# First transfers in written order, two squares behind their step's exponents, and own banks for the last halves of an attention and mixer kernel

## The chip, the core and the metric

The kernel runs on one core of a Trainium2 chip. The core has five engines that each take their own instructions in order: TensorE (PE, matmuls; its weight loads are listed as PEld), VectorE (DVE), ScalarE (ACT), GpSimd (POOL) and SyncE (SP, which issues DMAs).[...] The metric is the device time of one execution in microseconds (us), as the median of several executions.

## The reference

```python
# q, k, v: (8, 12, 448, 64), float32; g_q, g_k: (64,)
q_n, k_n = rmsnorm(q, g_q), rmsnorm(k, g_k)      # x / sqrt(mean(x * x) + 1e-6) * g
scores = q_n @ k_n.T / 8                         # for each batch and head
attn = softmax(scores)
x = (attn @ v), laid out as (8, 448, 768)
# w_tok1 (448, 256), w_tok2 (256, 448), w_ch1 (768, 1536), w_ch2 (1536, 768), float64
h = maximum(x.T @ w_tok1, 0) @ w_tok2
u = x + h.T
out = u + maximum(u @ w_ch1, 0) @ w_ch2          # (8, 448, 768)
```

The weights arrive as float64 and are turned into float32 by the kernel itself, from their two 32-bit words.

## The kernel before

**Units of work.** Two heads make a pair: with 64 dimensions each they fill the 128 partitions. There are 48 pairs, numbered from 0; two pairs share a "step group" `t`, so each group of four heads passes through four steps (`att_step(g)`, L650, with `t, s = divmod(g, 4)`). In a group the 448 keys are taken in seven blocks of 64. Step 0 makes the scores of block 0, steps 1 to 3 those of two blocks each (`score`, L444, matmuls at L452, exponents on ACT at L456), and from step 1 on PE also multiplies earlier blocks' exponents with the values (`values`, L525; row sums at L505). The score tiles come from a pool of four PSUM banks (`s_tile`), the other products from a pool of two (`m_tile`).

**Norms.** The norm of a pair is prepared by `square` (ACT, L1416), `reduce` (DVE, L1432), `roots` (a guess and three Newton steps, DVE or POOL) and `scale` (DVE, L1483). Then PE transposes the pair (`turn_qk`, L426), and ACT copies the result out of PSUM. In a step, the list `ahead` is issued before the step's scores and exponents, the list `behind` after them. In the first group, `turn_qk` of pairs 2 and 3 stands in step 3, between the scores and the values.

**Start.** Before the main body, the class `Start` (L1293) loads the queries and keys of pairs 0 to 3 (`load_qk`, L1377: two DMAs for the queries, two for the keys, 112 KB each) into parts of the tile `hb`. The keys of pairs 0 and 1 are issued by ACT, the rest by SP. Then it squares, reduces and scales pairs 0 and 1. Ahead of it, the kernel function loads the two gain vectors into one partition (L1516, L1517) and computes from them on DVE whether scores may grow large (L1521 to L1524). A branch on that value (`tc.If`, L1526) chooses between two bodies, `whole(tc, True, ...)` and `whole(tc, False, ...)`; with these inputs the second one runs. ACT's first activation is a one-column square (L1322), in front of which stands the load of its function table.

**Order.** PE, DVE, ACT and POOL run in written order in the whole kernel (`manual_schedule`, L1512). SP is not in that set[...].[...]

**Mixer.** Each batch's 448 by 768 result passes through the token mixing and then the channel mixing. The channel products use fewer block products than a plain multiplication: seven for the first (`ch1`, L996), fifteen forms for the second (`ch2`, L1052, matmuls at L1062). Each form `f` has two halves, `x` = 0 and 1, of 224 columns in one PSUM bank; after `x` = 1 the form's result is added to `uT` (L1077) on DVE or POOL. In the last batch the last form (f = 14) is treated apart: each half is added directly to the left half of one row block of `uT`, block 1 or block 4 (L1081). While a batch is mixed, the attention of the following batch is interleaved with it.

**End.** In the last batch, four of the six row blocks of `uT` are turned on DVE (L1090) and stored (L773). The last two, 1 and 4, go through `turn_last` (L1092): PE transposes (L1099) the right half (`lo` = 2), an engine copies it out of the bank (L1102, L1104), a DMA stores it (L1105), and then the same for the left half (`lo` = 0), in the same bank.

Of the kernel before, what the change touches and what calls it, by code (L numbers as in the profile page):

```python
# [8 lines left out]
F32 = mybir.dt.float32  # L9
# [14 lines left out]
NF9 = 15  # L24
# [59 lines left out]
def whole(ctx, tc, shifted, pre, q, k, v, g_q, g_k, moe_w_tok1, moe_w_tok2, moe_w_ch1, moe_w_ch2, out):  # L84


    nc = tc.nc
    B, H, S, D = q.shape
    C = H * D
    DT = moe_w_tok1.shape[1]  # L90
# [559 lines left out]
    def att_step(g):  # L650
# [54 lines left out]
        ahead, sooner, behind, turns = [], [], [], []  # L705
        f = lambda fn, *pairs: [lambda i=i: fn(i, st) for i in pairs]
        scales = lambda n: [lambda i=i: scale(i) for i in (n, n + 1)]
        if g in (1, 5):
            ahead, behind = f(pre.square, g // 4 * 2 + 4), f(pre.reduce, g // 4 * 2 + 4)
        elif g in (2, 6):  # L710
            ahead, behind = f(pre.square, g // 4 * 2 + 5), f(pre.reduce, g // 4 * 2 + 5)
        elif g in (3, 7):
            behind = pre.roots(g // 4 * 2 + 4, st)
        elif g in (4, 8):
            behind = scales(g // 4 * 2 + 2)
# [336 lines left out]
    def ch2(b, f, x):  # L1052

        put_off_done()
        if x == 0:
            st["m"] = m_tile()
        ps = st["m"]
        for i in range(4):
# [30 lines left out]
        t = st["y", cc] = turn_pool.tile([P, S], F32, name="turned")  # L1089
        nc.vector.transpose(out=t[:], in_=st["uT", b][:, cc, :])  # L1090

    def turn_last(b, cc, eng):  # L1092

        ps = s_tile("t_ps")
        t = cv_sb[:, cc // KC].rearrange("r (c n) -> r c n", c=NS)
        dst = out[b][:, cc * P:(cc + 1) * P].rearrange("(c r) n -> r c n", r=R)
        for lo in (HN, 0):
            for c in range(lo, lo + HN):
                nc.tensor.transpose(ps[0:R, c * P:(c + 1) * P], st["uT", b][:, cc, c * R:(c + 1) * R], ident[:])  # L1099
            part = ps[0:R, lo * P:(lo + HN) * P].rearrange("r (c n) -> r c n", c=HN)  # L1100
            if lo and cc == 1:
                nc.scalar.copy(out=t[0:R, lo:lo + HN], in_=part)  # L1102
            else:
                nc.vector.tensor_copy(out=t[0:R, lo:lo + HN], in_=part)  # L1104
            eng.dma_start(out=dst[:, lo:lo + HN], in_=t[0:R, lo:lo + HN])  # L1105

    def turns(b, cs, send=True):

# [65 lines left out]
    def last_items(b, items):  # L1174

        if ending(b):
            l = [(0.3, lambda cc=cc: (trans_y(b, cc), send_y(b, cc, st.pop(("y", cc))))) for cc in y_order(b)[:4]]
            last = [(0.1, lambda: turn_last(b, 1, nc.sync)), (0.1, lambda: turn_last(b, 1 + KC, nc.scalar))]
            return (items[:4] + l[0:1] + items[4:6] + l[1:2] + items[6:11] + l[2:3] + items[11:12] + l[3:4]
                    + items[12:] + last)  # L1180
        l = turns(b, y_order(b)[:4], not in_next(b))
        if b == 1:
            return merge(items, l)
        return items[:2] + [l[0]] + items[2:5] + [l[1]] + items[5:8] + [l[2]] + items[8:10] + [l[3], items[10]]
# [108 lines left out]
class Start:  # L1293


    def __init__(self, ctx, tc, q, k, g_q, g_k, w2):
        self.nc = nc = tc.nc
        self.q, self.k = q, k
        B, H, S, D = q.shape
# [19 lines left out]

        warm = const.tile([P, 1], F32, name="warm")  # L1320
        nc.vector.memset(warm[:], 1.0)
        nc.scalar.activation(out=warm[:], in_=warm[:], func=AF.Square)  # L1322
        self.load_qk(0, self.st, other=nc.scalar)
        self.load_qk(1, self.st, other=nc.scalar)
        self.g_t = const.tile([P, 2], F32, name="g_t")
        for i, g in enumerate((g_q, g_k)):
            for a in range(2):
# [164 lines left out]
@with_exitstack  # L1492
def kernel(
    ctx: ExitStack,
    tc: tile.TileContext,
    q: bass.AP,
    k: bass.AP,
    v: bass.AP,
    g_q: bass.AP,
    g_k: bass.AP,  # L1500
    moe_w_tok1: bass.AP,
    moe_w_tok2: bass.AP,
    moe_w_ch1: bass.AP,
    moe_w_ch2: bass.AP,
    out: bass.AP,
):


    nc = tc.nc
    D = q.shape[-1]  # L1510
    args = (q, k, v, g_q, g_k, moe_w_tok1, moe_w_tok2, moe_w_ch1, moe_w_ch2, out)
    ctx.enter_context(tc.manual_schedule(engines={  # L1512
        e.engine for e in (nc.tensor, nc.vector, nc.scalar, nc.gpsimd)}))
    gate = ctx.enter_context(tc.tile_pool(name="gate", bufs=1))
    g2 = gate.tile([1, 2, D], F32, name="g2")
    nc.sync.dma_start(out=g2[:, 0, :], in_=g_q.rearrange("(o d) -> o d", o=1))  # L1516
    nc.scalar.dma_start(out=g2[:, 1, :], in_=g_k.rearrange("(o d) -> o d", o=1))  # L1517
    gg = gate.tile([1, D], F32, name="gg")
    most = gate.tile([1, 1], F32, name="most")
    large = gate.tile([1, 1], I32, name="large")  # L1520
    nc.vector.tensor_tensor(out=gg[:], in0=g2[:, 0, :], in1=g2[:, 1, :], op=ALU.mult)  # L1521
    nc.vector.tensor_tensor(out=gg[:], in0=gg[:], in1=gg[:], op=ALU.mult)
    nc.vector.tensor_reduce(out=most[:], in_=gg[:], axis=AX_X, op=ALU.max)
    nc.vector.tensor_scalar(large[:], most[:], SCORE_BOUND**2 / D, None, ALU.is_gt)  # L1524
    pre = Start(ctx, tc, q, k, g_q, g_k, moe_w_ch2)
    with tc.If(nc.values_load(large[0:1, 0:1], min_val=0, max_val=1,  # L1526
                              skip_runtime_bounds_check_because="a comparison's result") > 0) as arm:
        whole(tc, True, pre, *args)
    with arm.Else():
        whole(tc, False, pre, *args)  # L1530
# [30 lines left out]
```

## Time and profile before

| | |
|---|---|
| Median of three runs | 1285.62 us (1283.6 to 1289.3) |
| Profiled execution, own time | 1289.21 us |
| Its span, first to last instruction | 1287.4 us |
| PE busy | 1253.8 us (97%) |
| DVE busy | 798.1 us (62%) |
| ACT busy | 392.7 us (31%) |
| POOL busy | 386.8 us (30%) |
| DMA | 228.37 MB, mean 177 GB/s |
| Chain that ended last | PE 86%, DVE 4%, DMA 4%, SP's queue 2%, ACT 1% |
| Mean granted PE clock | 0.995 |

All of it comes from one profiled execution. The span counts from the first to the last instruction; the execution's own time has some 1.8 us around it. "Busy" leaves out what an engine's queue does alone: waiting, branching and issuing DMAs. A line number names the line of the kernel before. A row of a view in order of time gives start, duration, engine, line, operation, what it writes and reads, its shape, a count, and in brackets how long the engine stood idle before it and what released it. A wait for several semaphores is put down to the one that came last, which can be a wait of another instruction just before.

### The profile page before, as it was taken

What the parts mean: (1) busy time and instruction counts of PE and PEld (TensorE: products, weight loads), DVE (VectorE), ACT (ScalarE), POOL (GpSimd) and SP (SyncE); (2) the same over time, 40 slices, a digit from 0 to 9 for tenths busy, and PEclk for the clock granted to TensorE, in tenths of its full rate; (3) what the DMA queues carried; (4) which work ended last, traced back from release to release, by engine and by line L of the source; (5) the groups of instructions that cost most, each with busy time, mean ns of one, the idle gap of its engine ahead of it and who ended that gap; (6) DMA issues with size and microseconds to landing.
All of it is one profiled execution on the core that took longest, in us unless ns stands there. A gap on an engine that the chain in (4) does not pass through costs nothing.

```text
span 1287.4 us, 20019 instructions
## 1 busy us (share of the span) xinstructions
PE 1253.8 (97%) x7236; PEld 889.2 (69%) x7236; DVE 798.1 (62%) x1243; ACT 392.7 (31%) x783; POOL 386.8 (30%) x629
## 2 busy tenths in 40 slices
PE   4999999999999999999999999999999999999997
PEld 2444444447744477796788768885887867797997
DVE  6889878846774255864668356765558456554233
ACT  3664333223331044302443034311343024300210
POOL 1112443024896612331133122241122322131222
PEclk9999999999999899999999999999999999999999
DMA  8676595999799867595657867595866864386554
GB/s 160 178 197 176 142 248 141 213 243 243 222 264 231 190 160 170 143 247 118 160 162 158 208 142 185 133 216 126 189 156 150 228 137 137 118 209 153 178 172 92
DMA packets 490112, 228.37 MB, mean 177 GB/s; under 512 B 371860, under 2 KB 450580, under 8 KB 490004
## 3 DMA queue, kind: packets, MB, share of 16 engines
q1 hardware_dynamic: 483154, 214.13, 67.4%
q0 software_dynamic: 3584, 12.06, 3.0%
q10 hardware_dynamic: 3266, 0.80, 0.3%
q8 instruction: 59, 0.97, 0.3%
q14 instruction: 49, 0.40, 0.1%
HBM read 184.26 MB, written 42.66 MB: 176 GB/s over the span
## 4 chain that ended last, share of the span: by engine, by line
PE 86%; DVE 4%; DMA 4%; SPq 2%; ACT 1%; issue 1%; DVEq 0%; ACTq 0%
PE m_ps L996 25%; PE m_ps L1062 21%; PE s_ps L452 9%; PE o_ps L525 9%; PE m_ps L876 5%; PE m_ps L966 5%; PE m_ps L1045 4%; PE m_ps L834 2%; PE t_ps L834 2%; PE d_ps L505 1%; DMA raw<-wp 1%; PE m_ps L505 1%; DVE raw L345 1%; DVE raw L343 1%; DMA x<-xs 1%
## 5 line engine op out<-in xcount | busy, mean ns | idle before, releaser
L1062 PE MATMUL m_ps<-hb,unit 128*128 128x224 f32 x1440 | 277.5, 354 | 1.2 <-DVE uT L1081 1.2
L1062 PEld LDWEIGHTS m_ps<-hb,unit 128*128 128x128 f32 x1440 | 270.9, 190 | 10.4 <-issue 7.5
L996 PE MATMUL m_ps<-tu,unit 128*128 128x224 f32 x1008 | 201.6, 355 | 1.3 <-ACT r L1006 1.3
L996 PEld LDWEIGHTS m_ps<-tu,unit 128*128 128x128 f32 x1008 | 189.1, 190 | 15.0 <-issue 9.2
L456 ACT ACTIVATE e<-s_ps 128x448 f32<-128x448 f32 x294 | 138.5, 553 | 178.4 <-PE s_ps L452 170.1
L996 PE MATMUL m_ps<-uT,unit 128*128 128x224 f32 x756 | 151.2, 354 | 0.1
L996 PEld LDWEIGHTS m_ps<-uT,unit 128*128 128x128 f32 x756 | 142.2, 190 | 7.2 <-issue 3.9
L452 PE MATMUL s_ps<-qkT 64*64 64x448 f32 x1260 | 143.8, 545 | 0.8 <-ACT x L816 0.8
L525 PE MATMUL o_ps<-e,v 64*64 64x448 f32 x1148 | 130.2, 539 | 0.3 <-ACT uT L562 0.2
L493 DVE TENSOR_TENSOR es<-es,e 128x896 f32<-128x896 f32 x90 | 104.8, 1165 | 12.5 <-ACT e L456 7.8
L1002 DVE TENSOR_TENSOR hb<-m_ps,r 128x448 f32<-128x448 f32 x63 | 39.1, 621 | 109.5 <-POOL r L1002 57.3
L1002 POOL TENSOR_TENSOR hb<-r,r 128x448 f32<-128x448 f32 x21 | 23.9, 1140 | 245.3 <-ACT r L1018 245.3
L452 PEld LDWEIGHTS s_ps<-qkT 64*64 64x64 f32 x1260 | 44.9, 132 | 70.1 <-issue 59.7
L525 PEld LDWEIGHTS o_ps<-e,v 64*64 64x64 f32 x1148 | 45.5, 133 | 64.2 <-issue 60.7
L1462 POOL TENSOR_TENSOR nt<-rs 128x56 f32<-128x56 f32 (+1 forms) x54 | 21.6, 400 | 202.9 <-DVE rs L1454 200.1
L1003 ACT ACTIVATE hb<-hb 128x448 f32<-128x448 f32 x84 | 48.4, 577 | 102.0 <-DVE hb L1002 77.9
L876 PE MATMUL m_ps<-w_sb,h 128*128 128x448 f32 x192 | 75.2, 544 | 0.5 <-DVE uT L881 0.5
L317 POOL TENSOR_TENSOR raw<-raw 128x128 f32<-128x128 f32 x128 | 65.8, 534 | 32.8 <-DMA raw<-wp 28.3
L1077 POOL TENSOR_TENSOR uT<-uT,r 128x448 f32<-128x448 f32 x42 | 51.5, 1241 | 78.3 <-DVE r L1077 46.6
L1432 DVE TENSOR_REDUCE ms<-sq 128x28 f32<-128x896 f32 (+2 forms) x44 | 47.5, 1080 | 35.9 <-ACT sq L1419 24.8
L1002 DVE TENSOR_TENSOR r<-m_ps,r 128x448 f32<-128x448 f32 x42 | 26.1, 622 | 64.2 <-PE m_ps L996 64.2
L881 DVE TENSOR_TENSOR uT<-uT,m_ps 128x448 f32<-128x448 f32 x48 | 29.3, 614 | 56.8 <-PE m_ps L876 56.8
(146 smaller groups left out, 1601.7 us busy)
## 6 DMA issues: line engine op xcount, KB each, us to landing
unit<-ws SPq DMA_DIRECT2D x267, 384.0 KB, 4.1
raw<-in_moe_w_ch_dram SPq DMA_DIRECT2D x72, 256.0 KB, 3.5
v<-in_v_dram SPq DMA_DIRECT2D x96, 112.0 KB, 3.6
out_dram<-turned SPq DMA_DIRECT2D x182, 56.0 KB, 2.0
xs<-xt SPq DMA_DIRECT2D x56, 168.0 KB, 4.6
qk_t<-in_q_dram SPq DMA_DIRECT2D x144, 56.0 KB, 3.4
qk_t<-in_k_dram SPq DMA_DIRECT2D x144, 56.0 KB, 3.5
x<-xs SPq DMA_DIRECT2D x42, 192.0 KB, 3.8
```

The source lines that it names most:

```text
L317: nc.gpsimd.tensor_tensor(out=at[o], in0=at[x], in1=at[y], op=ALU.add if op == "+" else ALU.subtract)
L452: nc.tensor.matmul(out=pss[i][rows_of(i, a), 0:S], lhsT=qkT[h, 1, k * D:(k + 1) * D], rhs=qkT[h, 0, :], start=True, stop=True)
L456: nc.scalar.activation(out=e[:, i, :], in_=pss[i][:, 0:S], func=AF.Exp)
L493: nc.vector.tensor_tensor(out=es[:], in0=(es if k > 1 else st["e", t, 0])[:], in1=st["e", t, k][:], op=ALU.add)
L525: nc.tensor.matmul(out=st["o", p][a * D:(a + 1) * D, 0:S], lhsT=vt[rows, k * D:(k + 1) * D], rhs=e[rows, :], **kw)
L834: nc.tensor.matmul(out=st["t1", h][jc][:, 0:HC], lhsT=w1_sb[:, c, jc * P:(jc + 1) * P], rhs=st["x", b, h][:, :, c, :], start=start and c = ...
L876: nc.tensor.matmul(out=ps[:, 0:S], lhsT=st["h1", jc][:, cc * P:(cc + 1) * P], rhs=w2_sb[:, jc].rearrange("p c r -> p (c r)"), start=(jc == ...
L966: nc.tensor.matmul(out=ps, lhsT=a[:, o + 2 * half, :], rhs=natural(half * KF + t) if wide else u[:, half * KC + t, :], start=(t == 0 and h ...
L996: nc.tensor.matmul(out=ps[:, j * HS:(j + 1) * HS], lhsT=w[:, t, j, :], rhs=m, start=(t == 0), stop=(t == KC - 1))
L1002: add = lambda e, o, x, y: e.tensor_tensor(out=o, in0=x, in1=y, op=ALU.add)
L1062: nc.tensor.matmul(out=ps[:, x * HS:(x + 1) * HS], lhsT=st["w"][:, tile_at % 6, :], rhs=hb[:, X_SLOT[f], i, :], start=(i == 0), stop=(i == 3))
L1077: e.tensor_tensor(out=get(out), in0=get(x_), in1=get(y), op=ALU.add if op == "+" else ALU.subtract)
```

## The change

It has three parts.

*First transfers.* While `Start` runs, SP is in the set of engines that keep written order as well. The set with four engines is entered again inside `whole`. The two gain loads stay first. The gain computation on DVE moves into `Start`, behind the issue of the loads of pairs 0 and 1, and so does ACT's one-column square; its memset on DVE now comes before the gain computation.

*Squares.* In steps 1 and 2 of the first group, the squares of pairs 4 and 5 move from `ahead` to `behind`, in front of their reduces. Steps 5 and 6 keep the old order.

*Last halves.* In the last form of the last batch, the half `x` = 1 takes a bank of its own. `turn_last` takes a bank for each half, writes both halves of the bank's columns from 0, and no longer names one engine for its DMAs: three of the four copies are ACT's, the left half of block 4 is copied by DVE; the right half of block 4 is stored by ACT's queue, the other three by SP's.

```diff
@@ -85,6 +85,9 @@
 
 
     nc = tc.nc
+    ctx.enter_context(tc.manual_schedule(engines={
+        e.engine for e in (nc.tensor, nc.vector, nc.scalar, nc.gpsimd)}))
+
     B, H, S, D = q.shape
     C = H * D
     DT = moe_w_tok1.shape[1]
@@ -705,9 +708,11 @@
         ahead, sooner, behind, turns = [], [], [], []
         f = lambda fn, *pairs: [lambda i=i: fn(i, st) for i in pairs]
         scales = lambda n: [lambda i=i: scale(i) for i in (n, n + 1)]
-        if g in (1, 5):
+        if g in (1, 2):
+            behind = f(pre.square, 3 + g) + f(pre.reduce, 3 + g)
+        elif g == 5:
             ahead, behind = f(pre.square, g // 4 * 2 + 4), f(pre.reduce, g // 4 * 2 + 4)
-        elif g in (2, 6):
+        elif g == 6:
             ahead, behind = f(pre.square, g // 4 * 2 + 5), f(pre.reduce, g // 4 * 2 + 5)
         elif g in (3, 7):
             behind = pre.roots(g // 4 * 2 + 4, st)
@@ -1052,7 +1057,7 @@
     def ch2(b, f, x):
 
         put_off_done()
-        if x == 0:
+        if x == 0 or ending(b) and f == NF9 - 1:
             st["m"] = m_tile()
         ps = st["m"]
         for i in range(4):
@@ -1089,20 +1094,21 @@
         t = st["y", cc] = turn_pool.tile([P, S], F32, name="turned")
         nc.vector.transpose(out=t[:], in_=st["uT", b][:, cc, :])
 
-    def turn_last(b, cc, eng):
-
-        ps = s_tile("t_ps")
+    def turn_last(b, cc):
+
         t = cv_sb[:, cc // KC].rearrange("r (c n) -> r c n", c=NS)
         dst = out[b][:, cc * P:(cc + 1) * P].rearrange("(c r) n -> r c n", r=R)
         for lo in (HN, 0):
-            for c in range(lo, lo + HN):
-                nc.tensor.transpose(ps[0:R, c * P:(c + 1) * P], st["uT", b][:, cc, c * R:(c + 1) * R], ident[:])
-            part = ps[0:R, lo * P:(lo + HN) * P].rearrange("r (c n) -> r c n", c=HN)
-            if lo and cc == 1:
+            ps = s_tile("t_ps")
+            for c in range(HN):
+                at = (lo + c) * R
+                nc.tensor.transpose(ps[0:R, c * P:(c + 1) * P], st["uT", b][:, cc, at:at + R], ident[:])
+            part = ps[0:R, 0:HN * P].rearrange("r (c n) -> r c n", c=HN)
+            if cc >= KC and lo == 0:
+                nc.vector.tensor_copy(out=t[0:R, lo:lo + HN], in_=part)
+            else:
                 nc.scalar.copy(out=t[0:R, lo:lo + HN], in_=part)
-            else:
-                nc.vector.tensor_copy(out=t[0:R, lo:lo + HN], in_=part)
-            eng.dma_start(out=dst[:, lo:lo + HN], in_=t[0:R, lo:lo + HN])
+            (nc.scalar if cc >= KC and lo else nc.sync).dma_start(out=dst[:, lo:lo + HN], in_=t[0:R, lo:lo + HN])
 
     def turns(b, cs, send=True):
 
@@ -1175,7 +1181,7 @@
 
         if ending(b):
             l = [(0.3, lambda cc=cc: (trans_y(b, cc), send_y(b, cc, st.pop(("y", cc))))) for cc in y_order(b)[:4]]
-            last = [(0.1, lambda: turn_last(b, 1, nc.sync)), (0.1, lambda: turn_last(b, 1 + KC, nc.scalar))]
+            last = [(0.1, lambda cc=cc: turn_last(b, cc)) for cc in (1, 1 + KC)]
             return (items[:4] + l[0:1] + items[4:6] + l[1:2] + items[6:11] + l[2:3] + items[11:12] + l[3:4]
                     + items[12:] + last)
         l = turns(b, y_order(b)[:4], not in_next(b))
@@ -1293,7 +1299,7 @@
 class Start:
 
 
-    def __init__(self, ctx, tc, q, k, g_q, g_k, w2):
+    def __init__(self, ctx, tc, q, k, g_q, g_k, w2, g2, gate):
         self.nc = nc = tc.nc
         self.q, self.k = q, k
         B, H, S, D = q.shape
@@ -1319,9 +1325,16 @@
 
         warm = const.tile([P, 1], F32, name="warm")
         nc.vector.memset(warm[:], 1.0)
-        nc.scalar.activation(out=warm[:], in_=warm[:], func=AF.Square)
         self.load_qk(0, self.st, other=nc.scalar)
         self.load_qk(1, self.st, other=nc.scalar)
+        nc.scalar.activation(out=warm[:], in_=warm[:], func=AF.Square)
+        gg = gate.tile([1, D], F32, name="gg")
+        most = gate.tile([1, 1], F32, name="most")
+        self.large = large = gate.tile([1, 1], I32, name="large")
+        nc.vector.tensor_tensor(out=gg[:], in0=g2[:, 0, :], in1=g2[:, 1, :], op=ALU.mult)
+        nc.vector.tensor_tensor(out=gg[:], in0=gg[:], in1=gg[:], op=ALU.mult)
+        nc.vector.tensor_reduce(out=most[:], in_=gg[:], axis=AX_X, op=ALU.max)
+        nc.vector.tensor_scalar(large[:], most[:], SCORE_BOUND**2 / D, None, ALU.is_gt)
         self.g_t = const.tile([P, 2], F32, name="g_t")
         for i, g in enumerate((g_q, g_k)):
             for a in range(2):
@@ -1509,20 +1522,14 @@
     nc = tc.nc
     D = q.shape[-1]
     args = (q, k, v, g_q, g_k, moe_w_tok1, moe_w_tok2, moe_w_ch1, moe_w_ch2, out)
-    ctx.enter_context(tc.manual_schedule(engines={
-        e.engine for e in (nc.tensor, nc.vector, nc.scalar, nc.gpsimd)}))
     gate = ctx.enter_context(tc.tile_pool(name="gate", bufs=1))
-    g2 = gate.tile([1, 2, D], F32, name="g2")
-    nc.sync.dma_start(out=g2[:, 0, :], in_=g_q.rearrange("(o d) -> o d", o=1))
-    nc.scalar.dma_start(out=g2[:, 1, :], in_=g_k.rearrange("(o d) -> o d", o=1))
-    gg = gate.tile([1, D], F32, name="gg")
-    most = gate.tile([1, 1], F32, name="most")
-    large = gate.tile([1, 1], I32, name="large")
-    nc.vector.tensor_tensor(out=gg[:], in0=g2[:, 0, :], in1=g2[:, 1, :], op=ALU.mult)
-    nc.vector.tensor_tensor(out=gg[:], in0=gg[:], in1=gg[:], op=ALU.mult)
-    nc.vector.tensor_reduce(out=most[:], in_=gg[:], axis=AX_X, op=ALU.max)
-    nc.vector.tensor_scalar(large[:], most[:], SCORE_BOUND**2 / D, None, ALU.is_gt)
-    pre = Start(ctx, tc, q, k, g_q, g_k, moe_w_ch2)
+    with tc.manual_schedule(engines={
+            e.engine for e in (nc.tensor, nc.vector, nc.scalar, nc.gpsimd, nc.sync)}):
+        g2 = gate.tile([1, 2, D], F32, name="g2")
+        nc.sync.dma_start(out=g2[:, 0, :], in_=g_q.rearrange("(o d) -> o d", o=1))
+        nc.scalar.dma_start(out=g2[:, 1, :], in_=g_k.rearrange("(o d) -> o d", o=1))
+        pre = Start(ctx, tc, q, k, g_q, g_k, moe_w_ch2, g2, gate)
+        large = pre.large
     with tc.If(nc.values_load(large[0:1, 0:1], min_val=0, max_val=1,
                               skip_runtime_bounds_check_because="a comparison's result") > 0) as arm:
         whole(tc, True, pre, *args)
```

## The prediction

> **What bounds the kernel now.** I read the page first (its head and part 1):
>
> ```profile
> span 1287.4 us, 20019 instructions
> ## 1 busy us (share of the span) xinstructions
> PE 1253.8 (97%) x7236; PEld 889.2 (69%) x7236; DVE 798.1 (62%) x1243; ACT 392.7 (31%) x783; POOL 386.8 (30%) x629
> ```
>
> TensorE (PE) is without work for only 33.6 us, so an edit pays only where PE stands still or runs slowly. Listing PE's gaps gives 16.72 us before its first matmul, 2.10 at 25.66, then none over 0.40 until 86.97; about 8 in all up to 430; and 1.22, 0.46 and 1.05 in the last ten. The edit touches the first two and the last three. Next, the instructions in order of time, 0 to 25 us (start, duration, engine, what, idle before it and its releaser; a q marks a queue issue):
>
> ```profile
> 1.31 1.28 ACT L1322 ACT_TABLE_LOAD   x1 [1.31 <-PEq L1545]
> ...
> 3.09 5.04 ACTq L1393 DMA_DIRECT2D hb<-in_k_dram  x4
> ...
> 12.17 0.63 ACT L1416 ACTIVATE qk_t<-hb 112x512 f32<-112x512 f32 x1 [0.97 <-DMA hb<-in_k_dram]
> ...
> 16.72 3.22 PE L426 MATMUL t_ps<-ident,hb 112*128 112x112 f32 x16 [16.72 <-DVE hb L1483]
> ```
>
> ACT begins its four key loads at 3.09, behind the table load and the warm-up, and needs 5.04 us for issues of 0.32 to 0.49 each.[...] The last key load of pair 1 stands behind a load of pair 2 that landed at 7.79, so it is issued at 7.82 and lands at 12.09. From there a fixed chain leads to PE: square, reduce, ten small operations, first scale, transpose: 16.72 - 12.09 = 4.63 us.
>
> The same view, 25 to 75 us:
>
> ```profile
> 26.21 1.06 ACT L1416 ACTIVATE sq<-hb 112x1024 f32<-112x1024 f32 x1 [3.08 <-DMA hb<-in_k_dram]
> ...
> 27.75 3.06 PE L452 MATMUL s_ps<-hb 64*64 64x448 f32 x16 [2.10 <-ACT e L456]
> ...
> 31.92 1.06 ACT L1416 ACTIVATE hb<-hb 112x1024 f32<-112x1024 f32 x1 [2.92 <-DMA hb<-in_k_dram]
> ...
> 36.08 1.75 PE L426 MATMUL t_ps<-ident,hb 112*128 112x112 f32 x16
> ```
>
> ACT takes its queue in order: the square of the fifth pair (number 4) waits for keys that land at 26.03, and the exponents of step 1 stand behind it; at 31.92 the sixth pair (landed 31.82) does it again. And in half-microsecond stretches:
>
> ```profile
> 29.00:29.50 0.50, 0.50 (x8) 0.34 (x6) 0.50 (x2) 0.00 (x1) 0.00 (x0) 0.50 1.36 206
> ```
>
> The third number from the right is PE's clock: half, for 3.41 us from 28.94. Last, 1255 us to the end:
>
> ```profile
> 1278.98 1.78 PE L1062 MATMUL m_ps<-hb,unit 128*128 128x224 f32 x8 [1.22 <-DVE uT L1081]
> ...
> 1281.44 0.65 PE L1099 MATMUL t_ps<-ident,uT 128*112 128x128 f32 x4 [0.46 <-ACT cv_sb L1102]
> ...
> 1283.14 0.43 PE L1099 MATMUL t_ps<-ident,uT 128*112 128x128 f32 x2 [1.05 <-DVE cv_sb L1104]
> 1283.61 0.42 DVE L1104 COPY cv_sb<-t_ps 112x256 f32<-112x256 f32 x1 [0.52 <-PE t_ps L1099]
> ```
>
> Each half waits until VectorE (DVE) or ACT has read the other half of the same bank. The last store is issued at 1284.06 and has landed at 1286.03.
>
> [...] The trace: 171 GB/s at 4 to 6 us, 254 at 6 to 8, then 174.[...] The trace at the If: ACT 12.72 to its next work at 15.45, SP 13.11 to 15.91, about 2.8 us with the DMA engines nearly idle, but PE 3.66 to 9.49 and POOL 4.38 to 10.09, some 5.8 us, under load.[...]
>
> **Part 1, first transfers.** Nothing is added: four ACT issues move ahead of the table load (1.28) and warm-up (0.20), four DVE gate operations (0.8 us) behind a memset, and SP keeps to written order.[...] ACT has issued all by about 3.3, and is through table load and warm-up by 4.8, before pair 0 can be whole; DMA hides both. Eight times 112 KB is 0.92 MB. With 136 GB/s (the 2 to 4 us rate) for a microsecond from 2.2, then an estimated 230, between the 171 and the 254, it lands at 3.2 + 0.78/0.23 = 6.6; pair 2's queries share the end: 7.0, bounds 6.3 to 8.3. Plus 4.63: PE can start at 11.6 to 12.0 (the small gain loads of POOL landed at 6.80, and DVE needs them between its reduces). PE's own branch, over at 9.5, has 2 us of cover.
>
> What is late next is ACT and SP behind their branches. SP's last load waits for pair 1, so is issued at about 7.5; ACT's last square ends at 7.7. Their branches at about 8.2 meet the rest of pairs 2 and 3, so I take 3.8 us, between 2.8 and 5.8. SP's first load inside is at 12.0 instead of 15.91, 3.9 us earlier (bounds 1.9 to 4.9). ACT, at 12.0, squares pair 2 (1.06) to 13.1, where the first transposes are done at 12.8: 0.3 us lost, up to 2.3 with the slow fetch.
>
> **Part 2, squares behind exponents.** Two instructions move on ACT; the two reduces stay behind them on DVE. In step 1 ACT stood idle 3.08 us, so four exponents (1.83) fit in: the 2.10 us gap and the half clock after it (3.41/2 = 1.7) go, 3.8 us. But the sixth pair is late next. PE would reach step 3's scores about 3.5 us earlier than 33.75, at 30.2, and end them at 31.7 on the scale of before; its transposes need score banks that step 3's exponents free, and those are now behind the square that waits until 31.82. So: 31.85 + 1.06 = 32.9, exponents 32.9 to 34.8, transposes done at 35.2 instead of 37.83: 2.6 us gained, and a new stop of about 1.7 us. As this path hangs on SP's loads, SP's shift counts, not PE's: 3.9 + 2.6 = 6.5 us by the end of step 3 (bounds 4.5 to 7.5). Below that, half a clock window (1.7) may be charged again. Later loads have cover: pairs 6 and 7 landed at 42.3 and 45.9 and are squared at 47.77 and 50.41. From there PE has work nearly without gaps, so what is won stays.
>
> **Part 3, tail.** Four matmuls of the last half (eight records of 0.19) follow at once: done at 1279.27 instead of 1280.77. Two transposes of the untouched right half follow; the rest need no copy. ACT has two store issues until 1279.6, then three copies of 0.37: 1280.0, 1280.35, 1280.7. DVE ends its add at 1279.7, PE the last transposes at 1280.05, DVE's copy at 1280.5. Three stores on SP, one on ACT, last issue about 1280.8. But SP's first may draw the semaphore of the store that ACT issues at 1278.68, landed 1281.0: then 1281.8. Against 1284.06 the gain is 2.3 to 3.2; I take 2.5. Moving three copies to ACT costs nothing: it is idle there.
>
> Sum: 3.9 + 2.6 + 2.5 = 9.0 us. The profiled execution took 1289.21 around its span of 1287.4; that becomes 1278.4 and 1280.2. The median of the three runs, 1285.62, is 3.6 lower; less the same 9.0, it gives 1276.6, on its own 1273.5 to 1279.5.
>
> **Rivals.** (a) *Only half arrives.* Fetch under load takes 5.8 us on ACT and SP: SP's shift is 1.9, ACT gives 2 us away, and the stop before step 3's transposes costs a half-clock window. 1.9 + 2.6 - 1.7 + 2.3 = 5.1: 1280.5. For it: PE's and POOL's 5.8. Against: by 10.5 the 1.8 MB are in, and fetches after that are quick. (b) *More.* Fetch 2.8 us, the loads pack at 254 GB/s, tail 3.2: 4.9 + 2.8 + 3.2 = 10.9, so 1274.7, and 1271.3 where the half clock at 431.71 (6.83 us in this execution, worth 3.4) doesn't come. (c) *The start does not move:*[...] pair 1 stands behind pair 2, or transfer time alone rules. Then parts 2 and 3 alone, 2.6 + 2.5: 1280.5, or the tail alone, 1283. Against: the rate of 89 GB/s at 10 to 12 us shows DMA engines waiting for issues. (d) *Slower.* SP inside `whole` is not bound to written order[...]. A unit load displaced until it is needed costs PE its 4.1 us from issue to landing; from four such (16.4 against the 9.0) the kernel is over 0.5% slower: 1293.0. Against: SP's order inside was the written one for the first 30 us.
>
> **How the numbers follow.** Forecast 0.55, (a) 0.20, (b) 0.13, (c) 0.08, (d) 0.04. A measurement here tells about 0.5% (6.4 us) from no change; the three runs differ by 5.7. Faster by over 0.5% means under 1279.2: nearly all of the forecast, (b), and a third of (a) and (c), 0.72; same 0.24; slower 0.04. The range 1271.5 to 1283 leaves out (d) and edges on both sides.
>
> **What would show it.** Right: PE's first matmul near 12; ACT's four key issues done by 3.5; no gap at step 1, but one of 1 to 2 us before the step-3 transposes with the sixth pair's load as cause; no wait on L1081 or on copies at the end; from the end of the second-last half (1277.75 now) to the end of the span about 7.1 us instead of 9.6. Wrong: ACT's first work after the If later than 13; pair 1's landing beyond 9; half-clock stretches in new places; unit loads as releasers of PE.

## The result, and the profile after

The changed kernel takes 1283.16 us (median of 22 executions, 1280.81 to 1287.31) beside 1288.31 us of the kernel before in the same runs (22 executions): a ratio of 0.9966, 95% interval 0.9955 to 0.9977. By this ratio it is 4.4 us less (3.0 to 5.8); the two medians lie 5.15 us apart. The forecast was 9.0 us less. Its level of 1276.6 us was low for a second reason: it started from 1285.62, the median of three, and the median of 22 executions is 2.7 us higher.

The head of the page after:

```profile
span 1282.0 us, 20022 instructions
## 1 busy us (share of the span) xinstructions
PE 1251.6 (98%) x7236; PEld 890.8 (69%) x7236; DVE 795.3 (62%) x1241; ACT 393.3 (31%) x785; POOL 387.9 (30%) x629
```

This execution took 1283.78 us, and its span is 5.4 us shorter than that of the profile before. From here on a line number names the line of the kernel that is profiled. In order of time, the start (columns as before: start, duration, engine, what, idle before it and its releaser):

```profile
1.30 1.96 ACTq L1406 DMA_DIRECT2D hb<-in_k_dram  x4
...
3.29 1.28 ACT L1330 ACT_TABLE_LOAD   x1 [3.29 <-issue]
...
6.86 1.98 SPq L1406 DMA_DIRECT2D hb<-in_q_dram  x2
7.56 1.15 ACT L1429 ACTIVATE qk_t<-hb 112x512 f32<-112x512 f32 x2 [0.89 <-DMA hb<-in_q_dram]
...
12.77 3.22 PE L429 MATMUL t_ps<-ident,hb 112*128 112x112 f32 x16 [12.77 <-DVE hb L1496]
13.41 1.46 SPq L408 DMA_DIRECT2D v_first<-in_v_dram  x2
```

ACT's four key loads are out by 3.26, ahead of the table load; pair 1 has landed at 7.84, not 12.09, and PE starts at 12.77 instead of 16.72. SP's first load inside `whole` (the last row) comes at 13.41 instead of 15.91: 2.5 us earlier, where 3.9 were forecast. Step 3 of the first group:

```profile
29.23 1.06 ACT L1429 ACTIVATE hb<-hb 112x1024 f32<-112x1024 f32 x1 [2.11 <-DMA hb<-in_k_dram]
...
30.20 0.74 ACT L356 ACTIVATE raw<-raw,expo_c 128x512 uint32<-128x512 uint32 x1
...
30.84 1.82 ACT L459 ACTIVATE e<-s_ps 128x448 f32<-128x448 f32 x4
...
31.41 3.25 PE L429 MATMUL t_ps<-ident,hb 112*128 112x112 f32 x16 [3.27 <-ACT e L459]
...
34.59 0.59 PE L528 MATMUL o_ps<-e,v_first 64*64 64x448 f32 x2
```

The stop of 2.10 us at step 1 is gone. In its place PE stands for 3.27 us ahead of the step-3 transposes, whose banks wait for ACT: the sixth pair's square (29.23, its keys landed at 29.13), then a weight conversion (L356), then the exponents. The transposes then take 3.25 us, not the 1.75 of before. Why is seen in stretches of 3.41 us, as long as the half-clock stretch in the records of this profile (31.20 to 34.61); such a stretch is called a window below. The second number is the time for which PE is busy; PE's granted clock is the third number from the right:

```profile
27.78:31.20 3.42, 0.37 (x2) 0.00 (x0) 3.32 (x6) 1.97 (x3) 0.00 (x0) 1.00 0.86 229
31.20:34.61 3.41, 3.20 (x19) 2.92 (x20) 3.19 (x6) 3.04 (x7) 0.00 (x0) 0.50 1.01 303
...
427.14:430.56 3.42, 0.72 (x4) 0.58 (x4) 0.00 (x0) 0.87 (x2) 3.26 (x9) 1.00 1.09 298
430.56:433.97 3.41, 3.41 (x7) 1.47 (x6) 0.65 (x1) 0.00 (x0) 3.27 (x8) 0.50 0.78 122
```

In both places a window in which PE hardly works (0.37 and 0.72 us of 3.42) is followed by one with a granted clock of 0.50. The end:

```profile
1275.78 1.07 PE L1105 MATMUL t_ps<-ident,uT 128*112 128x128 f32 x8
1275.98 0.39 DVE L1086 TENSOR_TENSOR uT<-uT,m_ps 128x224 f32<-128x224 f32 x1 [0.39 <-PE m_ps L1067]
1276.31 0.92 ACT L1110 COPY cv_sb<-t_ps 112x256 f32<-112x256 f32 x3 [11.86 <-PE t_ps L1105]
1276.71 1.88 SPq L1111 DMA_DIRECT2D out_dram<-cv_sb  x3
1276.89 0.42 DVE L1108 COPY cv_sb<-t_ps 112x256 f32<-112x256 f32 x1 [0.52 <-PE t_ps L1105]
1277.26 0.32 ACTq L1111 DMA_DIRECT2D out_dram<-cv_sb  x1
```

PE's eight transposes run without a gap; the waits of 1.22, 0.46 and 1.05 us are gone. SP's three stores take 1.88 us, because the second stands from 1277.03 to 1277.73 until a store that ACT issued at 1275.36 has landed.

Where the 5.43 us of the span come from:

| stretch | before | after | gain | forecast |
|---|---|---|---|---|
| start to the landing of the sixth pair's keys | 31.82 | 29.13 | 2.69 | 3.9 |
| landing to the values of step 3 | 5.94 | 5.46 | 0.48 | 2.6 |
| from there to the end of the second-last half | 1239.99 | 1239.84 | 0.15 | 0 |
| from there to the end of the span | 9.67 | 7.56 | 2.11 | 2.5 |

The third row came out near its forecast by luck. In the profiles of this section and the next that stretch takes 1235.7 to 1242.1 us, and PE's stops near 218 and 430 us with the half clock behind them differ from profile to profile. The profile before had a stop of 2.01 us and 6.83 us of half clock near 430, the one after 2.70 and 3.41. So the profiles are compared below also at a stop that all of them share, near 85 us, where PE waits 0.91 us for the same copy by ACT. Before, then after:

```profile
87.88 2.20 PE L834 MATMUL m_ps<-x,w_sb 128*128 128x384 f32 x6 [0.91 <-ACT x L814]
```

```profile
84.47 2.20 PE L839 MATMUL m_ps<-x,w_sb 128*128 128x384 f32 x6 [0.91 <-ACT x L819]
```

The changed kernel is 3.4 us ahead there (2.5 us in a second profile of it), where the prediction had 6.5 us by the end of step 3.

### The profile page after: what moved, and what is told of

Same layout as the page of the kernel before. It is cut to its first block, busy times and chain, and to the rows that moved or that the text cites. A ratio compares the mean times of both kernels' runs of the same rounds, so it can differ in the third digit from the quotient of the medians.

```text
span 1282.0 us, 20022 instructions
## 1 busy us (share of the span) xinstructions
PE 1251.6 (98%) x7236; PEld 890.8 (69%) x7236; DVE 795.3 (62%) x1241; ACT 393.3 (31%) x785; POOL 387.9 (30%) x629
## 4 chain that ended last, share of the span: by engine, by line
PE 86%; DVE 6%; DMA 2%; SPq 2%; issue 1%; ACT 1%; DVEq 0%; ACTq 0%
PE m_ps L1001 26%; PE m_ps L1067 21%; PE s_ps L455 9%; PE o_ps L528 8%; PE m_ps L881 5%; PE m_ps L971 5%; PE m_ps L1050 4%; PE m_ps L839 2%; PE t_ps L839 2%; PE d_ps L508 1%; DVE raw L346 1%; DVE raw L348 1%; DVE stage L379 1%; DMA raw<-wp 1%; PE m_ps L846 1%
```

## The experiments

The theory after the result was: the start moved as SP's queue allowed, the moved squares put the stop in another place, and the half clock that follows it took back most of part 2. The rival was that part 2 gained nothing at all, or that the start's gain was limited elsewhere. Each run was made beside the kernel before on the same chip, and ratios are to that kernel; its medians were 1289.32 to 1289.75 us where executions were repeated. A diff is against the changed kernel unless the text says otherwise.

**Parts alone.** First the change without its squares, that is with parts 1 and 3:

```diff
-        if g in (1, 2):
-            behind = f(pre.square, 3 + g) + f(pre.reduce, 3 + g)
-        elif g == 5:
+        if g in (1, 5):
             ahead, behind = f(pre.square, g // 4 * 2 + 4), f(pre.reduce, g // 4 * 2 + 4)
-        elif g == 6:
+        elif g in (2, 6):
             ahead, behind = f(pre.square, g // 4 * 2 + 5), f(pre.reduce, g // 4 * 2 + 5)
```

> The changed kernel with the squares of pairs 4 and 5 ahead of their step's exponents again (parts 1 and 3 alone). Theory A (the sixth pair's transfer sets the end of step 3, so moving the squares gave almost nothing): its keys land near 29.1, and the values of step 3 start 5.94 us later, as before: 35.1 against 34.6 in the changed kernel; the whole is 0.5 us slower than the changed one, 3.9 us faster than before. Rival B (part 2 gave its 2.6 us and the start gave less than it seems): the values start at 37.2 or later and the whole is at least 2.6 us slower than the changed kernel.

1285.43 us, ratio 0.9969 (0.9955 to 0.9983). The stop at step 1 is larger than ever, as PE now reaches it earlier:

```profile
25.77 3.69 PE L455 MATMUL s_ps<-hb 64*64 64x448 f32 x16 [4.39 <-ACT e L459]
```

Half clock lasts 6.83 us there, and the values start at 36.09, a microsecond later than theory A had it and 1.5 us later than with the squares moved. So part 2 is worth something beside part 1, though the executions alone can't tell (0.9969 here, 0.9966 with it). Over all profiles with the squares ahead, 5.94 to 6.33 us pass from the landing of the sixth pair's keys to the values (three profiles); over those with the two squares moved and nothing else changed there, 4.52 to 5.47 us (six). That is about 1 us for part 2, where 2.6 us were forecast. At the stop near 85 us this run is 1.9 us ahead of the kernel before. Next, the squares hunk of the change alone, on the kernel before:

> The kernel before with part 2 alone. Theory A: PE's gap of 2.10 us at 25.66 goes, a gap of about 3 us before the transposes of step 3 takes its place, half clock follows it, the values of step 3 start at 37.3 instead of 37.76; total 0 to 0.5 us faster. If the half clock stays away, 2 us. Rival B: the values start at 35.2, total 2.6 us faster.

1288.02 us, ratio 0.9990 (0.9977 to 1.0003). The stop moves from step 1 to the step-3 transposes (2.83 us), and its half window (35.56 to 38.98) moves with it. Values start at 36.51, 1.25 us earlier than before, but the next stop of PE is at 49.02 instead of 49.05: nothing is kept. The last part alone, on the kernel before:

```diff
-        if x == 0:
+        if x == 0 or ending(b) and f == NF9 - 1:
             st["m"] = m_tile()
...
+            ps = s_tile("t_ps")
...
```

> The kernel before with part 3 alone. Theory A: from the end of the second-last half to the landing of the last store 6.3 us instead of 8.3, no gap of PE in between, total 2.0 us faster. Of the forecast's 2.5 the rest is lost because SP's second store of block 1 waits for the semaphore of a store that ACT issued 2.3 us earlier. Rival: SP's issue rate sets it, then SP's stores follow each other at 0.35 us without such a wait.

1288.9 us, ratio 0.9994 (0.998 to 1.0008). By its profile the stretch from the end of the second-last half to the end takes 7.08 us instead of 9.67, 2.6 us less, so the part does what it says. The executions don't show it: their interval runs from 2.6 us less to 1.0 us more.

**What moved the start.** Part 1 has two halves. Without SP in the written order:

```diff
-            e.engine for e in (nc.tensor, nc.vector, nc.scalar, nc.gpsimd, nc.sync)}):
+            e.engine for e in (nc.tensor, nc.vector, nc.scalar, nc.gpsimd)}):
```

> Part 1 with ACT's order alone: the start's instructions keep their written order on PE, DVE, ACT and POOL, with ACT's key loads ahead of its table load and the gate computation behind them[...]. Theory A (ACT's four issues are the whole of the start): pair 1 lands at about 7.5 us, PE's first matmul starts at 12.8 as in the changed kernel and SP's first load behind the If at 13.4 to 14. Rival B[...]: SP's loads of pair 2 come between those of pair 1, pair 1 lands after 9 and PE starts at 14.5 or later.

PE starts at 13.05, pair 1 has landed at 8.11, SP is inside at 13.90. SP in written order, but with the gate computation and ACT's warm-up ahead of the loads:

```diff
+        gg = gate.tile([1, D], F32, name="gg")
...
+        nc.vector.tensor_scalar(large[:], most[:], SCORE_BOUND**2 / D, None, ALU.is_gt)
         warm = const.tile([P, 1], F32, name="warm")
         nc.vector.memset(warm[:], 1.0)
+        nc.scalar.activation(out=warm[:], in_=warm[:], func=AF.Square)
         self.load_qk(0, self.st, other=nc.scalar)
         self.load_qk(1, self.st, other=nc.scalar)
-        nc.scalar.activation(out=warm[:], in_=warm[:], func=AF.Square)
-        gg = gate.tile([1, D], F32, name="gg")
...
```

> The other half of part 1: SP in written order as well, but the gate computation, ACT's table load and its warm-up stand ahead of the loads again. Theory A: nothing of the start moves: pair 1 lands at about 12, PE's first matmul starts at 16.5 to 16.9, SP's first load behind the If at 15 to 16. Rival B: SP's order is what counts, and PE starts before 15.

PE starts at 17.41 and SP is inside at 15.60: nothing moved. ACT's rows of this run, in order of time:

```profile
1.30 1.28 ACT L1335 ACT_TABLE_LOAD   x1 [1.30 <-PEq L1552]
3.09 0.20 ACT L1335 ACTIVATE warm<-warm 128x1 f32<-128x1 f32 x1 [0.50 <-DVE warm L1334]
3.09 6.62 ACTq L1406 DMA_DIRECT2D hb<-in_k_dram  x4
...
12.87 0.63 ACT L1429 ACTIVATE qk_t<-hb 112x512 f32<-112x512 f32 x1 [1.44 <-DMA hb<-in_k_dram]
```

The four issues need 6.62 us. The last of them stands until 9.40, for a load of pair 2 that SP issued. So the move of ACT's loads ahead of its table load, with the gate behind them, is what moves the start, and SP's place in the set does nothing that these profiles show: over the eight profiles with SP in written order as well and the same loads, PE starts at 12.77 to 13.45 and SP is inside at 13.13 to 14.33. (These two runs, and the next where it is said, are single executions: 1285.79 and 1285.91 us beside 1291.36 of the kernel before. They are read by their profiles, not by these times.)

**Does SP's queue set the rest?** The loads of pair 3 move behind the branch:

```diff
+    pre.load_qk(3, st)
     load_v(0)
...
         self.load_qk(2, self.st)
-        self.load_qk(3, self.st)
```

> The changed kernel with the four loads of the fourth pair (number 3) moved from the start behind the If, ahead of the first value load. Theory A (SP's queue sets the sixth pair's landing): SP reads the branch's value at about 6.9 instead of 10.0 and is through its branch at about 9.8; the four loads take some 2.2 us there, so its first value load comes at 12.0 to 12.6 instead of 13.41, and the sixth pair's keys land 0.8 to 1.4 us earlier than 29.13, at 27.7 to 28.3, and the step-3 transposes begin as much earlier than 31.41. Rival B (the landing is set by the transfer rate of all 16 engines, not by the issue): the sixth pair lands within 0.4 us of 29.13.

1282.2 us, a single execution. SP is at the branch at 8.87 instead of 10.56 and issues its first load inside at 11.81, so the branch takes 2.94 and 2.85 us. But the loads of pair 3 then bring the value load to 13.83, later than the 12.0 to 12.6 of theory A, and further on the queue is ahead again without any use. SP's queue:

```profile
11.81 0.85 SPq L1406 DMA_DIRECT2D hb<-in_q_dram  x2
...
13.83 1.46 SPq L408 DMA_DIRECT2D v_first<-in_v_dram  x2
...
24.33 1.02 SPq L1406 DMA_DIRECT2D hb<-in_k_dram  x2
```

The sixth pair's last key load is issued at 24.87, 1.45 us earlier than in the changed kernel (26.32), and lands at 30.43, 1.3 us later. Near 85 us this run is only 0.3 us ahead of the kernel before. Four-microsecond stretches, first of the changed kernel, then of this run (the last two columns are the busy share of the DMA engines and GB/s):

```profile
24.00:28.00 4.00, 4.00 (x36) 1.48 (x27) 1.81 (x5) 2.80 (x5) 0.00 (x0) 1.00 0.73 178
```

```profile
24.00:28.00 4.00, 4.00 (x51) 1.56 (x42) 3.02 (x7) 2.79 (x5) 0.00 (x0) 1.00 1.22 227
```

In this run the share is 1.22 where the changed kernel has 0.73 (it counts overlapping packets, so it can pass 1), and that last key load takes 5.56 us from issue to landing instead of 2.81. Theory A fails here: from about 20 us on, what the earlier issue won (1.45 us) was lost again between issue and landing (2.75 us more). The run also puts the 448 KB of pair 3 behind the branch, which adds to what is under way there. The profiles that keep the changed kernel's order of loads say the same: in these eight the last key load of the sixth pair is issued anywhere from 24.95 to 26.91 and lands at 29.13 to 30.45, and those issued at 25.00 and 26.61 land at 29.63 and 29.75. One more run changes the bytes ahead of the sixth pair:

```diff
     for i in range(5):
+        if i == 1:
+            pre.load_qk(5, st)
         weight_load(i)
+        if i < 1:
+            pre.load_qk(4, st)
         if i < 2:
-            pre.load_qk(4 + i, st)
             load_v(2 + i)
```

> The changed kernel with the sixth pair's four loads issued ahead of the second weight chunk instead of behind it, so that 512 KB fewer stand before them; the squares stay behind the exponents as in the change. Theory A (from 20 us on the transfer itself sets when the sixth pair lands, as the run with the earlier queue showed, so what counts is the bytes ahead of it): 512 KB at 225 GB/s is 2.3 us, so the keys land at 26.6 to 27.6 instead of 29.13 to 29.63; the square is over before 28.7, the transposes of step 3 start at 28.9 to 29.4 at full clock, the standstill ahead of them is under 1.2 us with no half clock behind it, and the values of step 3 start at 30.7 to 31.3 instead of 34.5. DVE is late next: its conversions wait 2 us longer for the second chunk, which brings back stops of 1 to 2 us by 50 us; 2 to 4 us less than the changed kernel in all, ratio 0.993 to 0.996. Rival B (SP's issue sets it, and the other loads are no burden): the keys land less than 1 us earlier than 29.4, and the standstill and the half clock stay.

1281.62 us, ratio 0.9946 (0.9929 to 0.9963). ACT, then PE:

```profile
27.22 1.06 ACT L1432 ACTIVATE hb<-hb 112x1024 f32<-112x1024 f32 x1 [0.60 <-DMA hb<-in_k_dram]
28.18 0.73 ACT L356 ACTIVATE raw<-raw,expo_c 128x512 uint32<-128x512 uint32 x1
28.82 1.83 ACT L459 ACTIVATE e<-s_ps 128x448 f32<-128x448 f32 x4
```

```profile
29.39 1.91 PE L429 MATMUL t_ps<-ident,hb 112*128 112x112 f32 x16 [1.75 <-ACT e L459]
31.23 0.59 PE L528 MATMUL o_ps<-e,v_first 64*64 64x448 f32 x2
```

The keys land by 27.2 and the values start at 31.23, both as theory A said: with 512 KB fewer in front the keys land 1.9 us earlier than in the changed kernel. The last key load is also issued earlier, at 23.10, so this run alone doesn't tell bytes from issue; that issues 24.95 to 26.91 made no difference above is what speaks for the bytes. The standstill is 1.75 us and not under 1.2, since the conversion (L356) still stands between square and exponents. No half clock follows, and from landing to values it takes 4.0 us instead of 5.46. Near 85 us this run is 5.2 us ahead of the kernel before.

**The half clock.** The score products of step 3 are issued several times over, into the same banks, so that PE has work where it stood:

```diff
-        for i in range(2):
-            qkT = st["qkT", 2 * t + i]
+        for n in range(4 if t == 0 and k in (5, 6) else 1):
+            for i in range(2):
+                qkT = st["qkT", 2 * t + i]
...
```

> The changed kernel with the score products of step 3 issued four times over (the same product into the same bank, so 24 further matmul records, at 0.43 us for four about 2.6 us of PE work), which fills most of the 3.27 us in which PE stands ahead of the step-3 transposes, and delays nothing behind it, since ACT's exponents wait for the sixth pair's square until 30.8. Theory A (the standstill sets off the half clock): no half-clock stretch near 31 us; the transposes begin at 31.4 as in the changed kernel and take 1.75 to 1.9 us instead of 3.25, and the values of step 3 start at 33.1 to 33.4 instead of 34.59. Rival B (the half clock comes at that time whatever PE did just before): the transposes still take over 3 us, and the values start at 34.5 or later.

1279.97 us, a single execution. Four times was too often: it made 48 further records and not 24, the products ran until 33.1 and held up the exponents, so the values started at 34.83, which is rival B's range and not theory A's. But the transposes took 1.75 us, and no half clock came, as theory A said. Hence three times, with 3 in place of 4 in that line:

> The score products of step 3 issued three times over instead of four: four times was 48 further records and 4.3 us of PE, more than the standstill, so the exponents were held up by the products. 32 further records are 2.9 us, within the 3.27. Theory A (the standstill sets off the half clock): no half-clock stretch near 31 us, transposes in 1.75 to 1.9 us, and from the landing of the sixth pair to the first value product 4.0 to 4.3 us instead of 5.46. Rival B: the transposes take over 3 us, and 5.3 us or more pass from the landing to the values.

```profile
25.94 4.94 PE L456 MATMUL s_ps<-hb 64*64 64x448 f32 x46
31.93 1.91 PE L429 MATMUL t_ps<-ident,hb 112*128 112x112 f32 x16 [1.05 <-ACT e L460]
33.77 0.59 PE L529 MATMUL o_ps<-e,v_first 64*64 64x448 f32 x2
```

From the landing (29.65) to the values 4.12 us instead of 5.46, transposes in 1.91 us, no half-clock window. More work on PE makes the stretch 1.3 us shorter. So of the 2.6 us forecast for step 3, about 1.3 went to the half clock in the profile after. This single execution took 1278.74 us; that it is 5 below the changed kernel's is not all from here: near 85 us it is 0.8 us ahead of that one, and it has no half clock at 430 us.

**Taking the stop away.** The square and the reduce of the sixth pair go behind step 3:

```diff
-        if g in (1, 2):
-            behind = f(pre.square, 3 + g) + f(pre.reduce, 3 + g)
+        if g == 1:
+            behind = f(pre.square, 4) + f(pre.reduce, 4)
...
+        elif g == 3:
+            behind = f(pre.square, 5) + f(pre.reduce, 5) + pre.roots(4, st)
...
```

> The changed kernel with the square and reduce of pair 5 one step later, behind step 3's exponents and transposes and ahead of the roots. Theory A: nothing in step 3 waits for the sixth pair any more; PE's gap of 3.27 us at 28.15 and the half clock behind it (1.5 us in the transposes) go; the values of step 3 start near 30 instead of 34.59; the whole is 3.5 to 4.8 us faster than the changed kernel, ratio to before 0.993. Rival C (transfers and the weight conversions hold the first 50 us anyway): the gap turns up again within ten microseconds, and the whole is as the changed kernel, ratio 0.9966.

1282.12 us, ratio 0.9953 (0.9939 to 0.9968). PE:

```profile
28.99 1.90 PE L429 MATMUL t_ps<-ident,hb 112*128 112x112 f32 x16
...
42.38 1.37 PE L508 MATMUL m_ps<-e,one_c 64*64 64x448 f32 x6 [1.00 <-DVE dt L557]
...
51.43 0.75 PE L429 MATMUL t_ps<-ident,hb 112*128 112x112 f32 x5 [1.28 <-ACT e L459]
```

The values start at 30.83, 3.8 us earlier than in the changed kernel, with no stop and no half clock. But DVE is late next: it had waited for weights, and its reading of the row sums (L557) and then a conversion ahead of the exponents stop PE for 1.00 and 1.28 us. Near 85 us the kernel is only 1.3 us ahead of the changed one (83.19 beside 84.47). The ratio lies between the two theories' 0.993 and 0.9966.

Last, this version with the left block of the last half stored by one DMA, and the changed kernel once more beside it:

```diff
-            (nc.scalar if cc >= KC and lo else nc.sync).dma_start(out=dst[:, lo:lo + HN], in_=t[0:R, lo:lo + HN])
+            if cc >= KC:
+                (nc.scalar if lo else nc.sync).dma_start(out=dst[:, lo:lo + HN], in_=t[0:R, lo:lo + HN])
+        if cc < KC:
+            nc.sync.dma_start(out=dst, in_=t[0:R])
```

> The kernel with the sixth pair's square and reduce behind step 3 (the version sixth_step3), and the left block of the last half stored by one DMA instead of two. Theory A (SP's second store only waits for the semaphore of a store that ACT issued earlier, and the third pays for it): the last store is issued 0.4 us earlier, so that from the end of the second-last half to the last landing it takes 5.9 us instead of 6.28; the ratio to the kernel before is 0.3 us better than sixth_step3's 0.9953, about 0.995, and 2 us better than the changed kernel's in the same call. Rival B (the merged store draws that semaphore itself and is twice as long): 6.2 us or more, and nothing gained over sixth_step3.

> The changed kernel as it is, for the comparison on the same chip: 4 to 5 us less than the kernel before (ratio 0.9966). Where the half-clock stretch in the records comes behind every standstill of two microseconds and more, it is there again behind the one at about 28 us; whether the standstill at about 427 us is as long (2.70 in the profile of the change, none in the version with repeated products) shows how far that one is the kernel's own.

The merged version takes 1280.11 us, ratio 0.9934 (0.9914 to 0.9954); the changed kernel 1285.66, ratio 0.9968 (0.9955 to 0.998). So a version that beats both was found: by the ratio 8.5 us less than before (its interval and that of the changed kernel just don't overlap). The merged store has no part in it: its last issue is indeed 0.4 us earlier (3.31 us after the second-last half instead of 3.73), but the end comes 7.10 us after that half, where sixth_step3 has 7.13. As rival B said, the merged store itself waits for ACT's store: that one has landed at 1273.18, and the merged one is issued at 1273.24. Why it measured 2 us better than sixth_step3 (0.9934 beside 0.9953, intervals that overlap) is left open; its profiled span is the longer of the two, 1277.0 beside 1276.3 us.

In this second profile of the changed kernel the stop before the transposes of step 3 is there again, with half clock from 32.80 on:

```profile
31.92 2.62 PE L429 MATMUL t_ps<-ident,hb 112*128 112x112 f32 x16 [3.37 <-ACT e L459]
```

Here the half clock began 0.88 us after the transposes had started, so part of its cost fell on the values behind them: 4.84 us from landing to values, not 5.46. The run also has a half-clock window more, at 220 us. Windows of it, then one of the run with ACT's order alone:

```profile
217.12:220.53 3.41, 1.48 (x5) 0.49 (x4) 3.34 (x7) 1.90 (x4) 0.08 (x1) 1.00 0.87 164
220.53:223.94 3.41, 3.41 (x5) 1.64 (x6) 3.38 (x3) 1.69 (x3) 2.70 (x2) 0.50 0.99 245
```

```profile
217.66:221.07 3.41, 1.58 (x5) 0.49 (x3) 3.31 (x8) 1.75 (x4) 0.00 (x0) 1.00 0.89 174
```

The window with 1.93 us of idle was followed by half clock; the one with 1.83 was not (that run's next half clock is at 432.70). The stop at 427 us was 2.70 us in the first profile and falls into two of 0.54 and 0.75 in this one: its length is not the kernel's own.

## Why the prediction was wrong, by its steps

Of the forecast 9.0 us the two profiles show 5.4. Missing are 1.2 us at the start, 2.1 in step 3 and 0.4 at the tail.

**What bounds the kernel, and the start of PE: right, with a small miss.** PE's first matmul was forecast at 11.6 to 12.0 and came at 12.77; the landing of pair 1 came at 7.84, forecast 7.0 (6.3 to 8.3). DVE stood 0.74 us for a small gain load that landed at 8.01. The reason given, that ACT's issues wait for landings of earlier loads, is shown by the trace before (the issue at 7.82 follows the landing at 7.79) and by the two halves of part 1: ACT's four issues are done by 3.27 with ACT's order alone, and at 9.71 without it.

**"SP's last load waits for pair 1, so is issued at about 7.5": failed, by 1.4 of the 3.9 us.** The load is issued at 9.43. On the way one load waits until 4.21 for a key load of ACT's, one until 5.97 for the next, and the issue at 6.86 takes 1.45 us instead of 0.5. So SP reaches its branch at 10.56 and not at 8.2. The branch itself was sized in the wrong direction, 2.85 us and not 3.8 (2.52 to 2.94 in all fourteen profiles), which gave 0.95 us back. The pair of profiles is a favourable one, too: SP is inside at 14.78 to 15.91 in the four profiles with the old start and at 13.13 to 14.33 in the nine with the new one and the same loads at the start, 1.6 us earlier on average, where 3.9 were forecast.

**"As this path hangs on SP's loads, SP's shift counts": failed as a rule.** In the four profiles with the old start the sixth pair has landed at 31.58 to 32.03, in the eight with the new one and the same loads at 29.13 to 30.45; the mean difference is 2.1 us. From 20 us on the landing doesn't follow SP's issue: an issue 1.45 us earlier gained nothing, the eight profiles show no relation of issue and landing, and 512 KB fewer in front gained 1.9 us. The prediction counted the shift of SP's queue in full, and it read the DMA rates only in the first 12 us.

**"Exponents 32.9 to 34.8, transposes done at 35.2": failed, the largest miss.** From the landing to the end of the transposes 3.35 us were forecast; it was 5.5. The weight conversion on ACT was not counted (0.65 us), and the half clock was put among the bounds (1.7 us, "may be charged again") though the sum itself held a stop of 1.7 us. Both could be read off the profile before. There the conversion already stands in ACT's queue behind the sixth pair's square (31.92) and right ahead of the exponents of step 3:

```profile
34.58 0.81 ACT L353 ACTIVATE raw<-raw,expo_c 128x512 uint32<-128x512 uint32 x1
35.27 1.85 ACT L456 ACTIVATE e<-s_ps 128x448 f32<-128x448 f32 x4
```

And the stop of 2.10 us, which ended at 27.75, was followed there by half clock (28.94 to 32.35). The stop of 1.7 us became 3.27, as PE came 4 us earlier and the keys only 2.7, with the conversion on top.

**The tail: right in mechanism, sized a little too large.** 2.1 us where 2.5 (2.3 to 3.2) were forecast. From the end of the second-last half to the end of the span, eleven profiles with this tail take 7.08 to 7.66 us and the two with the old one 9.30 and 9.67: 2.1 us less on average. The fear that a store of SP's waits for one of ACT's was right: it costs SP's second store 0.7 us (1277.03 to 1277.73).

**The baseline.** Three executions gave 1285.62 us; 22 gave 1288.31.

**Rivals.** (a), 5.1 us, had the right sum by a half-right road, so partly by luck: SP's shift was small and half clock came, but no branch took 5.8 us on ACT or SP (from the branch to the next work 2.98 us on ACT, 2.85 on SP). (b) fell: the branch did take 2.85 us, but SP was inside 2.5 us earlier and not 4.9, and the tail gave 2.1 and not 3.2. (c) fell with PE's start at 12.77, though its second reason, that transfer time rules, fits the sixth pair's keys (1.9 us earlier with 512 KB fewer in front). (d) fell: no unit load releases PE. What decided were two terms of the main sum, both too large: in these two profiles the start gave 2.7 us and not 3.9, and step 3 gave 0.5 and not 2.6.

## What to carry to other kernels

When a wait in an in-order queue is moved back, write down when its data lands, when the engine now gets there, and what else is queued between; the stop is the difference. In the trace before, the stop of 2.10 us on PE was followed by 3.41 us at half clock, up to 1.7 us more. The sixth pair's keys gained nothing here by an issue 1.45 us earlier (they landed 1.3 us later), and 1.9 us by 512 KB fewer in front: look at which bytes go first. A stop that is removed uncovers the next engine's, so read the whole stage and not the one wait.

## What the runs showed of the hardware

The half clock (0.50) came in stretches of 3.41 us and, at 431.71 in the trace before, of 6.83; why that one was longer is open. In the profiles compared here their starts lie whole multiples of 3.413 us apart: 118 of them between 28.94 and 431.71 in the trace before, 117 between 31.20 and 430.56 in the one after, 55 between 32.80 and 220.53 in the second profile of the changed kernel. PE's idle time in a window at full clock, and the granted clock in the window behind it:

| run | window | PE idle, us | clock behind it |
|---|---|---|---|
| after | 27.78 to 31.20 | 3.05 | 0.50 |
| act_only | 29.92 to 33.34 | 2.81 | 0.50 |
| after | 427.14 to 430.56 | 2.70 | 0.50 |
| before | 25.53 to 28.94 | 2.10 | 0.50 |
| after_again | 217.12 to 220.53 | 1.93 | 0.50 |
| before | 428.30 to 431.71 | 1.85 | 0.50 |
| act_only | 217.66 to 221.07 | 1.83 | 1.00 |
| two_more | 38.22 to 41.63 | 1.44 | 1.00 |
| before | 339.55 to 342.97 | 1.30 | 1.00 |
| after_again | 428.74 to 432.16 | 1.29 | 0.50 |
| act_only | 26.51 to 29.92 | 1.18 | 1.00 |

So the idle time of that window alone doesn't settle what follows: 1.29 us was followed by half clock, 1.83 us by full clock. The records of the clock begin at 22.11 us in the trace before and at 17.54 in the one after; what PE's earlier idle time did is not shown.

The same stop of the changed kernel didn't cost the same twice: with 3.27 us and half clock from 31.20 on, 5.46 us passed from landing to values, with 3.37 us and half clock from 32.80 on, 4.84. Such differences fit most of the spread: of the 22 executions of the changed kernel, those with a mean granted clock of 0.998 took 1281.75 us on average (8 of them), 0.997 1283.74 (7), 0.996 1285.06 (4), 0.995 1285.98 (1), 0.994 1287.19 (2). As an estimate, a half-clock stretch of 3.41 us costs 3.41/2 = 1.7 of 1283 us, or 0.0013 of mean clock. How many such stretches each execution had is not on record, so this is a fit and not a count.
